# Closing the early tiles from the last recurrence unit on, none of them beside the last two own tiles

## The chip, the cores and the metric

One core of a Trainium2 chip runs the kernel. The metric is the device time of one execution in microseconds (us). Each engine works through its own list of instructions in order: TensorE (PE) multiplies matrices into PSUM, VectorE (DVE) does the elementwise work and the scans, ScalarE (ACT) moves PSUM into SBUF with a scale, GpSimd (POOL) and SyncE (SP) mostly issue DMAs here. Engines wait for each other through semaphores.

## The reference

For an input `x` of 2048 tokens by 1024 channels in bf16, two branches are computed and mixed with a gate per token:

```python
g = sigmoid((x * gate_w).sum(-1, keepdims=True))
# branch A: a filter in the two-dimensional Fourier domain
a = irfft2(rfft2(x) * (w_r + 1j * w_i), s=(2048, 1024))
# branch B: a diagonal complex recurrence over the tokens
Lam_bar = exp(exp(log_dt) * Lam)
Bu = einsum("bld,pd->blp", x, ((Lam_bar - 1) / Lam)[:, None] * Bmat)
h_t = Lam_bar * h_{t-1} + Bu_t
b = 2 * einsum("bld,pd->bld", h, Cmat).real + x * Dskip
out = g * a + (1 - g) * b
```

(The second einsum contracts the 1024 states with `Cmat`.) The output is bf16, 2048 by 1024.

## The kernel before

**Tokens.** The output is made in 16 tiles of 128 tokens, numbered 0 to 15. The recurrence runs in 8 chunks `c` of 256 tokens, so tile `tb` needs the states of chunk `tb // 2`. A chunk's states are handled in two units, `unit(c, 0)` and `unit(c, 1)`, of 512 states each.

**A unit** (lines 251 to 306) has two halves, real and imaginary. A half is 32 matmuls on PE into a PSUM tile `psu` (L299) and one cast by ACT into `h` (L301). Its weights are the transposed B matrix, in the eight SBUF tiles `BT0` to `BT7`: the units with q = 0 read `BT0` to `BT3`, those with q = 1 read `BT4` to `BT7`. After the second half a unit puts seven pieces of DVE work on a list: `turn_back` (L260, L261), `join` (L266, L267, L269), two scans (L273), `carry_on` (L279 to L281), `turn` (L285, L286) and `join_on` (L291, L292). Only after `join_on` may PE use the unit's states. The order on PE, DVE and ACT is the order in which the program emits instructions. A call `vector(us)` emits pieces from the list until that many microseconds of them are spent; so the calls to `vector` set where DVE's pieces stand among its other work. SP's and POOL's queues are put in order by the scheduler.

**Tiles 0 to 9** are "early": their branch B is computed while branch A is still under way, scaled by 1 - g and written as float32 to `y_scratch` in DRAM (`early`, L574 to L580). They are closed late in the program. `late_tile` (L603) calls `spectral` (L585), which makes branch A for the tile: 8 matmuls into a PSUM tile `ps_id` (L591), one scaling by ACT (L594), four additions by DVE (L596, L597, L599, L600). Then POOL issues a DMA that adds the tile's `y_scratch` onto the result in SBUF (L605), and SP stores the sum (L613). The function `close(keep)` emits the stores of all closed tiles but the last `keep`. Here the home of the sum of tile `tb` is the whole of `BT[tb % 4]`: its first half holds the sum, its second half holds `eo`, the intermediate result of the additions. There are four homes.

**Tiles 10 to 15** are "own": `own_tile` (L615) computes branch B after branch A is ready. Each has two halves `hf` of 512 channels; each half is 16 matmuls over the states (L560) and 4 for the `Dskip` term (L564). Between its halves the program makes branch A of the next own tile (`spectral`, with a home in the tile `raw`). Tiles 10 to 13 add branch A with one more matmul (L567), and ACT writes the output (L625), which SP stores (L626). In tiles 14 and 15 DVE does the scaling and the addition for each half (L632), and SP stores each half (L634). The outputs lie in `BT[4 + tb % 4]`.

**PSUM.** Two pools matter. `psU` has two buffers that `psu`, the early `ps_y` and `ps_id` take in turn; `psA` has two that `ps_y` and `ps_h` of the own tiles take in turn. A matmul that starts a new tile waits until the tile two before it in the same pool has been read out.

**The last stage** (lines 899 to 918). The units (6, 1), (7, 0) and (7, 1) run first. Then five DMA transposes load `x` for tiles 11 to 15 over the free part of `xQ` (L910). Then come own tiles 10 to 15, and after each half of tiles 10 to 14 one early tile is closed, tiles 0 to 9 in order: the last two, 8 and 9, after the two halves of tile 14. `close(1)` is called before each.

Of the kernel before, what the change touches and what calls it, by code (L numbers as in the profile page):

```python
# [20 lines left out]
D = 1024  # L21
# [85 lines left out]
def kernel(  # L107
# [75 lines left out]
    BT = [btp.tile([P, 2, 8, P], BF16, name=f"BT{jb}") for jb in range(8)]  # L183
# [60 lines left out]
    def halloc(shape, dtype):  # L244
        pool = hpool[hcount[0] % (NHA + NHB) >= NHA]
        hcount[0] += 1
        return pool.tile(shape, dtype, name="h")
# [3 lines left out]
    def unit(c, q):  # L251
        sh = [P, 2, 4, TC]
        u = halloc(sh, BF16)
        js = slice(4 * q, 4 * q + 4)
        bc = lambda i: tab[:, i:i + 1, js, :].to_broadcast(sh)
        tmps = {}

        def turn_back():
            su = up.tile(sh, BF16, name="su")
            nc.vector.tensor_mul(out=su, in0=u[:, ::-1], in1=bc(1))  # L260
            nc.vector.tensor_mul(out=u, in0=u, in1=bc(0))  # L261
            tmps["su"] = su

        def join():
            su = tmps["su"]
            nc.vector.tensor_add(out=u[:, 0], in0=u[:, 0], in1=su[:, 0])  # L266
            nc.vector.tensor_sub(out=u[:, 1], in0=su[:, 1], in1=u[:, 1])  # L267
            if c:
                nc.vector.tensor_add(out=u[:, :, :, 0], in0=u[:, :, :, 0], in1=carry[:, :, js])  # L269

        def scan(ri):
            seg = u[:, ri].rearrange("p j t -> p (j t)")
            nc.vector.tensor_tensor_scan(out=seg, data0=rz[:, js].rearrange("p j t -> p (j t)"), data1=seg,  # L273
                                         initial=0.0, op0=ALU.mult, op1=ALU.add)

        def carry_on():
            if c + 1 < NCH:
                gl = u[:, :, :, TC - 1]
                nc.vector.tensor_mul(out=ck[:, 0, :, js], in0=gl, in1=cTC[:, js].unsqueeze(1).to_broadcast([P, 2, 4]))  # L279
                nc.vector.tensor_mul(out=ck[:, 1, :, js], in0=gl[:, ::-1], in1=sTC2[:, :, js])  # L280
                nc.vector.tensor_add(out=carry[:, :, js], in0=ck[:, 0, :, js], in1=ck[:, 1, :, js])  # L281

        def turn():
            sg = up.tile(sh, BF16, name="sg", tag="su")
            nc.vector.tensor_mul(out=sg, in0=u[:, ::-1], in1=bc(3))  # L285
            nc.vector.tensor_mul(out=u, in0=u, in1=bc(2))  # L286
            tmps["sg"] = sg

        def join_on():
            sg = tmps["sg"]  # L290
            nc.vector.tensor_add(out=u[:, 0], in0=u[:, 0], in1=sg[:, 0])  # L291
            nc.vector.tensor_sub(out=u[:, 1], in0=u[:, 1], in1=sg[:, 1])  # L292
            hs[c, q] = u

        for ri in range(2):
            psu = pools["u"].tile([P, 4, TC], FP32, name="psu", tag="psu")
            for j in range(4):
                for d8 in range(8):
                    nc.tensor.matmul(psu[:, j, :], lhsT=BT[4 * q + j][:, ri, d8, :],  # L299
                                     rhs=xQ[:, d8, :, 16 * c:16 * (c + 1)], start=(d8 == 0), stop=(d8 == 7))  # L300
            nc.scalar.copy(out=u[:, ri].rearrange("p b (q j) -> p b q j", j=16),  # L301
                           in_=psu.rearrange("p b (j q) -> p b q j", j=16))
            if ri == 1:
                work.extend([(2.4, turn_back), (1.5, join), (2.3, lambda: scan(0)), (2.3, lambda: scan(1)),
                             (0.5, carry_on), (2.4, turn), (1.4, join_on)])
            yield 3.5
# [3 lines left out]
    def vector(us):  # L310
        owed[0] += us
        while work and owed[0] > 0:
            cost, piece = work.pop(0)
            piece()
            owed[0] -= cost
        if not work:
            owed[0] = min(owed[0], 0.0)
# [264 lines left out]
    own_home = lambda tb: raw[:, 2 * D * (tb % 2):2 * D * (tb % 2 + 1)]  # L582
    flat = lambda t: t.rearrange("p r j m -> p (r j m)")

    def spectral(tb, scale, home):  # L585
        ZT_t = fft["ZT"]
        pse = pools["u"].tile([P, 4, H], FP32, name="ps_id", tag="psu")
        for slot, (cls, ri) in enumerate(((0, 0), (1, 1), (0, 1), (1, 0))):
            for kb in range(2):
                i = 4 * cls + 2 * kb + ri  # L590
                nc.tensor.matmul(pse[:, slot, :], lhsT=ZT_t[:, i, tb, :], rhs=fft["Gi"][:, i, :],  # L591
                                 start=(kb == 0), stop=(kb == 1))
        part = home[:, 0:D].rearrange("p (s c n) -> p s c n", s=2, c=2)
        nc.scalar.activation(out=part.rearrange("p s c n -> p (s c) n"), in_=pse, func=ACT.Copy, scale=scale[:, tb:tb + 1])  # L594
        eo = home[:, D:2 * D].rearrange("p (c k) -> p c k", c=2)
        nc.vector.tensor_add(out=eo[:, :, 0:H], in0=part[:, 0], in1=part[:, 1])  # L596
        nc.vector.tensor_sub(out=eo[:, :, K - 1:H - 1:-1], in0=part[:, 0], in1=part[:, 1])  # L597
        ga = part.rearrange("p s c n -> p s (c n)")
        nc.vector.tensor_add(out=ga[:, 0], in0=eo[:, 0], in1=eo[:, 1])  # L599
        nc.vector.tensor_sub(out=ga[:, 1], in0=eo[:, 0], in1=eo[:, 1])  # L600
        return ga, eo

    def late_tile(tb):  # L603
        ga, _ = spectral(tb, gB, flat(BT[tb % 4]))
        nc.gpsimd.dma_start(out=ga, in_=y_dram[tb].rearrange("h p n -> p h n"), accum_op=ALU.add)  # L605
        closing.append((tb, ga))

# [2 lines left out]
    def close(keep):  # L610
        while len(closing) > keep:
            tb, ga = closing.pop(0)
            nc.sync.dma_start(out=out2[P * tb:P * (tb + 1), :], in_=ga.rearrange("p h n -> p (h n)"))  # L613
# [91 lines left out]
    gB = cpool.tile([P, 16], FP32, name="gB")  # L705
# [32 lines left out]
    def chain(*items):  # L738
        for item in items:
            yield from item  # L740

    def halves(gen, n):
        for _ in range(n):
            next(gen, None)
# [151 lines left out]
    ga = {}  # L896
    late = list(range(NEARLY))

    def own(tb):
        for v in own_tile(tb, ga.pop(tb)):  # L900
            if v == "half" and tb + 1 < 16:
                ga[tb + 1] = spectral(tb + 1, grat if tb + 1 < NSUM else gB, own_home(tb + 1))
            yield v

    ga[NEARLY] = spectral(NEARLY, grat, own_home(NEARLY))
    for _ in chain(unit(6, 1), unit(7, 0), unit(7, 1)):
        vector(4.0)
    for tb in range(NEARLY + 1, 16):
        xs[tb] = xQ.rearrange("p d (k j) m -> p (d k) (j m)", k=2)[:, tb].rearrange("p (d m) -> p d m", m=P)
        nc.sync.dma_start_transpose(out=xs[tb], in_=x[P * tb:P * (tb + 1), :])  # L910
    for tb, counts in ((10, (1, 1)), (11, (1, 1)), (12, (1, 1)), (13, (1, 1)), (14, (1, 1)), (15, (0, 0))):
        for _, n in zip(own(tb), counts):
            vector(4.0)
            for _ in range(n):
                close(1)
                late_tile(late.pop(0))
            if tb == 15:
                close(0)
    guard.__exit__(None, None, None)

# [29 lines left out]
```

## Time and profile before

| what | value |
|---|---|
| median of 5 runs | 356.61 us (355.51 to 361.84) |
| the profiled execution | 357.93 us |
| its span, first to last instruction | 356.1 us |
| mean granted TensorE clock | 0.993 |
| PE busy | 340.4 us (96%) |
| DVE busy | 292.6 us (82%) |
| ACT busy | 167.6 us (47%) |
| POOL busy | 34.2 us (10%) |

The span is what the views of the trace cover; 1.83 us of the profiled execution lie around it. PE is busy almost throughout, so what counts is where PE has to wait and what comes after its last matmul. In the forty slices of the page PE shows 9 tenths in nearly every slice up to the 39th and 2 tenths in the last one, which is 8.9 us long.

### The profile page before, as it was taken

What the parts mean: (1) busy time and instruction counts of PE and PEld (TensorE: products, weight loads), DVE (VectorE), ACT (ScalarE), POOL (GpSimd) and SP (SyncE); (2) the same over time, 40 slices, a digit from 0 to 9 for tenths busy, and PEclk for the clock granted to TensorE, in tenths of its full rate; (3) what the DMA queues carried; (4) which work ended last, traced back from release to release, by engine and by line L of the source; (5) the groups of instructions that cost most, each with busy time, mean ns of one, the idle gap of its engine ahead of it and who ended that gap; (6) DMA issues with size and microseconds to landing.
All of it is one profiled execution on the core that took longest, in us unless ns stands there. A gap on an engine that the chain in (4) does not pass through costs nothing.

```text
span 356.1 us, 6452 instructions
## 1 busy us (share of the span) xinstructions
PE 340.4 (96%) x2529; PEld 226.8 (64%) x2529; DVE 292.6 (82%) x477; ACT 167.6 (47%) x215; POOL 34.2 (10%) x66
## 2 busy tenths in 40 slices
PE   8989899899997999999999999999999999999992
PEld 4555476676966584747566665786958875655651
DVE  2659777999995999999999999969146999999850
ACT  3698668654232145657555541563533324434410
POOL 1372111200011000000000000000000000212420
PEclk9999999999999999999999999999999999999997
DMA  7999999997964047899999727844501024366795
GB/s 253 416 250 164 209 214 191 190 246 186 269 154 91 0 90 187 227 222 273 247 274 241 229 83 208 211 117 116 149 0 61 1 60 119 61 116 124 100 213 130
DMA packets 83742, 59.55 MB, mean 167 GB/s; under 512 B 54368, under 2 KB 74496, under 8 KB 83584
## 3 DMA queue, kind: packets, MB, share of 16 engines
q1 hardware_dynamic: 80400, 56.46, 62.1%
q0 software_dynamic: 3232, 2.67, 7.9%
q8 instruction: 20, 0.33, 0.4%
q14 instruction: 10, 0.08, 0.1%
q10 hardware_dynamic: 80, 0.01, 0.0%
HBM read 31.32 MB, written 17.84 MB: 138 GB/s over the span
## 4 chain that ended last, share of the span: by engine, by line
PE 68%; DVE 14%; DMA 8%; issue 3%; ACT 3%; SPq 1%; POOL 0%; ACTq 0%; DVEq 0%
PE ps_y L560 24%; PE psu L299 21%; PE ps_is L501 4%; PE ps_h L560 4%; PE ps_id L591 4%; DVE h L273 2%; PE ps_fd L334 2%; PE ps_s L452 2%; PE ps_is L477 2%; DMA G_sb<-c_G 2%; PE ps_is L476 2%; DMA col_scratch<-Acol 2%; DMA turn_scratch<-A 2%; PE ps_y L564 2%; DVE A L348 1%
## 5 line engine op out<-in xcount | busy, mean ns | idle before, releaser
L299 PE MATMUL psu<-xQ,BT 128*128 128x256 bf16 x1024 | 116.1, 273 | 3.7 <-ACT ye L578 2.4
L299 PEld LDWEIGHTS <-BT 128*128 128x128 bf16 x1024 | 100.2, 98 | 19.1 <-issue 4.5
L560 PE MATMUL ps_y<-CT,h 128*128 128x512 bf16 x448 | 101.4, 379 | 0.0
L560 PEld LDWEIGHTS <-h 128*128 128x128 bf16 x512 | 50.0, 98 | 55.3
L273 DVE TENSOR_TENSOR_SCAN h<-rz,h 128x1024 bf16<-128x1024 f32 x32 | 72.4, 2282 | 0.3
L301 ACT CAST h<-psu 128x1024 bf16<-128x1024 f32 x32 | 32.3, 1010 | 61.2 <-PE psu L299 61.2
L605 POOL DMA_DIRECT2D BT<-y_scratch x10 | 12.1, 1206 | 227.1 <-DMA out_dram<-BT 195.3
L334 PE MATMUL ps_fd<-G_sb,preT 128*128 128x512 bf16 x128 | 30.4, 379 | 2.1 <-ACT X L337 1.6
L260 DVE TENSOR_TENSOR su<-h,tab 128x2048 bf16<-128x2048 bf16 x16 | 19.6, 1223 | 14.0 <-ACT h L301 11.3
L578 ACT ACTIVATE ye<-ps_y,omg 128x512 f32<-128x512 f32 x20 | 12.6, 683 | 34.8 <-PE ps_y L564 22.7
L334 PEld LDWEIGHTS <-preT 128*128 128x128 bf16 x128 | 11.9, 97 | 15.5 <-issue 3.2
L454 ACT CAST X<-ps_s 128x1024 bf16<-128x1024 f32 x16 | 16.2, 1014 | 8.7 <-PE ps_s L452 8.7
L261 DVE TENSOR_TENSOR h<-h,tab 128x2048 bf16<-128x2048 bf16 x16 | 19.6, 1225 | 0.8
L337 ACT CAST X<-ps_fd 128x1024 bf16<-128x1024 f32 x16 | 16.2, 1013 | 8.4 <-PE ps_fd L334 8.4
L286 DVE TENSOR_TENSOR h<-h,tab 128x2048 bf16<-128x2048 bf16 x16 | 19.6, 1225 | 0.5
L285 DVE TENSOR_TENSOR sg<-h,tab 128x2048 bf16<-128x2048 bf16 x16 | 19.5, 1218 | 0.0
L503 ACT CAST ZT<-ps_is 128x1024 bf16<-128x1024 f32 x16 | 15.4, 1022 | 6.9 <-PE ps_is L501 3.5
L348 DVE CAST A<-ps_s 128x1024 bf16<-128x1024 f32 x10 | 12.2, 1222 | 6.2 <-PE ps_s L346 4.2
L646 ACT COPY xQ<-pt 128x1024 bf16<-128x1024 bf16 x16 | 15.9, 1019 | 2.3 <-PE pt L645 2.3
L479 ACT CAST C<-ps_is 128x1024 bf16<-128x1024 f32 x16 | 16.1, 1007 | 0.0
L591 PE MATMUL ps_id<-raw,ZT 128*128 128x256 bf16 x128 | 15.8, 273 | 0.0
L501 PE MATMUL ps_is<-KRS_sb,raw 128*128 128x128 bf16 x128 | 15.3, 311 | 0.0
(192 smaller groups left out, 403.9 us busy)
## 6 DMA issues: line engine op xcount, KB each, us to landing
y_scratch<-ye SPq DMA_DIRECT2D x20, 256.0 KB, 2.4
CT<-in_A_x_dram SPq DMA_DIRECT2D x8, 512.0 KB, 6.8
turn_scratch<-A SPq DMA_DIRECT2D x16, 256.0 KB, 3.4
Bb<-turn_scratch SPq DMA_DIRECT2D x16, 256.0 KB, 3.9
turn_scratch<-C SPq DMA_DIRECT2D x16, 256.0 KB, 3.0
raw<-turn_scratch SPq DMA_DIRECT2D x16, 256.0 KB, 3.7
Wb<-in_A_w_r_dram SPq DMA_DIRECT2D x32, 127.8 KB, 4.2
Wb<-in_A_w_i_dram SPq DMA_DIRECT2D x32, 127.8 KB, 3.6
```

What stands on the lines that cost most here:

```text
L260: nc.vector.tensor_mul(out=su, in0=u[:, ::-1], in1=bc(1))
L261: nc.vector.tensor_mul(out=u, in0=u, in1=bc(0))
L273: nc.vector.tensor_tensor_scan(out=seg, data0=rz[:, js].rearrange("p j t -> p (j t)"), data1=seg, initial=0.0, op0=ALU.mult, op1=ALU.add)
L285: nc.vector.tensor_mul(out=sg, in0=u[:, ::-1], in1=bc(3))
L286: nc.vector.tensor_mul(out=u, in0=u, in1=bc(2))
L299: nc.tensor.matmul(psu[:, j, :], lhsT=BT[4 * q + j][:, ri, d8, :], rhs=xQ[:, d8, :, 16 * c:16 * (c + 1)], start=(d8 == 0), stop=(d8 == 7))
L301: nc.scalar.copy(out=u[:, ri].rearrange("p b (q j) -> p b q j", j=16), in_=psu.rearrange("p b (j q) -> p b q j", j=16))
L334: nc.tensor.matmul(ps[:, cls, :], lhsT=preTs[j][:, 4 * cls + d4, :], rhs=G_sb[:, cls, d4, :], start=(d4 == 0), stop=(d4 == 3))
L337: nc.scalar.copy(out=X1.rearrange("p r (i c) -> p r i c", c=2), in_=ps.rearrange("p c (r i) -> p r i c", r=2))
L501: nc.tensor.matmul(pv[:, :, g::4], lhsT=Cq[:, g, P * kc:P * (kc + 1)], rhs=KRS_sb[:, 1, :], start=True, stop=True)
L560: nc.tensor.matmul(psy, lhsT=hs[c, jb // 4][:, ri, jb % 4, P * tq:P * (tq + 1)], rhs=CT[ri][:, jb, 512 * dh:512 * (dh + 1)], start=(i == 0 ...
L591: nc.tensor.matmul(pse[:, slot, :], lhsT=ZT_t[:, i, tb, :], rhs=fft["Gi"][:, i, :], start=(kb == 0), stop=(kb == 1))
```

## The change

The early tiles are closed sooner. One is closed after each half of `unit(7, 1)`, and one after each half of tiles 10 to 13; none is closed beside tiles 14 and 15. All ten are still closed in order.

The homes are smaller and there are six. A sum takes half of a `BT` tile: `BT0`, `BT1` and `BT2` have two slots each, and tile `tb` has slot `tb % 6`. The intermediate `eo` lies in one half of `BT3`, the halves being taken in turn. `close(2)` instead of `close(1)` is called before a tile is closed, and `close(0)` when no early tile is left. The instructions of `late_tile` and `spectral` are the same in kind, number and size.

In the emitted lists nothing differs before the second half of `unit(7, 1)`. From there on, each early tile stands two places earlier on PE, ACT and DVE. On DVE tiles 0 and 1 now stand before the pieces of `unit(6, 1)`'s `join_on` and after `unit(7, 0)`'s `turn_back`, and seven early tiles (0 to 6) instead of five stand before `join_on` of `unit(7, 1)`. The five transposes still stand ahead of all the stores in SP's queue. The end of that queue is below, each entry a store:

| | last stores in SP's queue, in order |
|---|---|
| before | tile 6, first half of 14, tile 7, second half of 14, tile 8, first half of 15, tile 9, second half of 15 |
| changed | tile 8, first half of 14, tile 9, second half of 14, first half of 15, second half of 15 |

```diff
--- before.py
+++ after.py
@@ -582,7 +582,7 @@
     own_home = lambda tb: raw[:, 2 * D * (tb % 2):2 * D * (tb % 2 + 1)]
     flat = lambda t: t.rearrange("p r j m -> p (r j m)")
 
-    def spectral(tb, scale, home):
+    def spectral(tb, scale, home, eo_home=None):
         ZT_t = fft["ZT"]
         pse = pools["u"].tile([P, 4, H], FP32, name="ps_id", tag="psu")
         for slot, (cls, ri) in enumerate(((0, 0), (1, 1), (0, 1), (1, 0))):
@@ -592,7 +592,7 @@
                                  start=(kb == 0), stop=(kb == 1))
         part = home[:, 0:D].rearrange("p (s c n) -> p s c n", s=2, c=2)
         nc.scalar.activation(out=part.rearrange("p s c n -> p (s c) n"), in_=pse, func=ACT.Copy, scale=scale[:, tb:tb + 1])
-        eo = home[:, D:2 * D].rearrange("p (c k) -> p c k", c=2)
+        eo = (home[:, D:2 * D] if eo_home is None else eo_home).rearrange("p (c k) -> p c k", c=2)
         nc.vector.tensor_add(out=eo[:, :, 0:H], in0=part[:, 0], in1=part[:, 1])
         nc.vector.tensor_sub(out=eo[:, :, K - 1:H - 1:-1], in0=part[:, 0], in1=part[:, 1])
         ga = part.rearrange("p s c n -> p s (c n)")
@@ -601,7 +601,8 @@
         return ga, eo
 
     def late_tile(tb):
-        ga, _ = spectral(tb, gB, flat(BT[tb % 4]))
+        slot = lambda i: flat(BT[i // 2])[:, D * (i % 2):D * (i % 2 + 1)]
+        ga, _ = spectral(tb, gB, slot(tb % 6), slot(6 + tb % 2))
         nc.gpsimd.dma_start(out=ga, in_=y_dram[tb].rearrange("h p n -> p h n"), accum_op=ALU.add)
         closing.append((tb, ga))
 
@@ -903,18 +904,27 @@
             yield v
 
     ga[NEARLY] = spectral(NEARLY, grat, own_home(NEARLY))
-    for _ in chain(unit(6, 1), unit(7, 0), unit(7, 1)):
+    last = unit(7, 1)
+
+    def close_early(n):
+        for _ in range(n):
+            close(2)
+            late_tile(late.pop(0))
+
+    for _ in chain(unit(6, 1), unit(7, 0)):
         vector(4.0)
+    for n in (1, 1):
+        halves(last, 1)
+        vector(4.0)
+        close_early(n)
     for tb in range(NEARLY + 1, 16):
         xs[tb] = xQ.rearrange("p d (k j) m -> p (d k) (j m)", k=2)[:, tb].rearrange("p (d m) -> p d m", m=P)
         nc.sync.dma_start_transpose(out=xs[tb], in_=x[P * tb:P * (tb + 1), :])
-    for tb, counts in ((10, (1, 1)), (11, (1, 1)), (12, (1, 1)), (13, (1, 1)), (14, (1, 1)), (15, (0, 0))):
+    for tb, counts in ((10, (1, 1)), (11, (1, 1)), (12, (1, 1)), (13, (1, 1)), (14, (0, 0)), (15, (0, 0))):
         for _, n in zip(own(tb), counts):
             vector(4.0)
-            for _ in range(n):
-                close(1)
-                late_tile(late.pop(0))
-            if tb == 15:
+            close_early(n)
+            if not late:
                 close(0)
     guard.__exit__(None, None, None)
```

## The prediction

> **What bounds the kernel now.** I read the view of the chain that ended last first, restricted to the last 15 us. Its columns are start, length, engine, tile and line.
>
> ```profile
> 340.86 0.87 PE ps_id L591 x8
> 341.74 3.45 PE ps_h L560 x16
> 345.19 0.22 PE ps_h L564 x4
> 345.41 3.45 PE ps_h L560 x16
> 348.87 0.24 PE ps_h L564 x4
> 349.10 0.02 issue
> 349.13 0.75 DVE BT L632
> ```
>
> PE works without a gap that matters: from 269.02 on each piece of this chain begins where the last ended, to a few tenths. Then comes DVE's last addition, done at 349.13 + 0.75 = 349.88. But the span is 356.1. The timeline of SP and of POOL for the same stretch shows what fills the other 6.2 us.
>
> ```profile
> 336.30 1.20 POOL L605 DMA_DIRECT2D BT<-y_scratch  x1 [0.27 <-issue]
> 341.08 1.20 POOL L605 DMA_DIRECT2D BT<-y_scratch  x1 [3.59 <-DVE BT L600]
> 346.10 1.20 POOL L605 DMA_DIRECT2D BT<-y_scratch  x1 [3.82 <-DVE BT L600]
> ...
> 343.63 0.33 SPq L613 DMA_DIRECT2D out_dram<-BT  x1
> ...
> 347.24 0.33 SPq L613 DMA_DIRECT2D out_dram<-BT  x1
> ...
> 352.64 0.33 SPq L613 DMA_DIRECT2D out_dram<-BT  x1
> 353.07 0.39 SPq L634 DMA_DIRECT2D out_dram<-BT  x1
> ```
>
> The last accumulating DMA (tile 9) is issued at 346.10, and its store goes out at 352.64, 6.54 later. The store of tile 15's second half stands behind it in SP's queue and goes out at 353.07, 3.19 us after its data was ready. From there 3.03 us remain to the end: 2.0 until the store lands (the shortest landing listed for L634), the rest the program's closing. The view of SP's own waits names the cause.
>
> ```profile
> SPq L613 <- DMA BT<-y_scratch: 44.1, 10, 7.5
> ```
>
> So two things set the end: PE's list up to 349.1, and one accumulation that ends after PE does.
>
> **Step 1, the tail.** In the changed list SP's last three entries are the halves of tiles 14 and 15, with no early store between or behind. The last store can start when its data is ready. Handing over from an engine to SP costs about 0.03 us where SP's queue is clear (ACT's L625 of tile 10 ended at 300.82, its store started at 300.85). Saved: 3.19 - 0.03 = **3.16 us**, if tile 9's sum is stored by then (step 4).
>
> **Step 2, a new wait on PE.** Before, the two halves of `unit(7, 1)` took different buffers of `psU`. Now tile 0's `ps_id` stands between them, so the second half takes the buffer of the first half again and must wait for ACT's cast of it. The trace has no such wait in this stretch, so I build it from rows. ACT's cast of this half is this one, in the timeline of ACT:
>
> ```profile
> 286.69 1.01 ACT L301 CAST h<-psu 128x1024 bf16<-128x1024 f32 x1 [2.48 <-PE psu L299]
> ```
>
> By the chain the half ends at 269.02 + 5 x 3.49 = 286.47, so ACT starts 0.22 later and needs 1.01. PE goes on some 0.05 after ACT is done (ACT ended at 268.97, PE began at 269.02). That is 1.28 us. Tile 0's 8 matmuls cover 0.87 of it. Left: **0.4 us** of stall, and everything on PE behind it is as much later. Its ends: 0, if the cast is not waited for, and 1.28, if the 8 matmuls hide nothing. I take 0.4, since all three terms are rows.
>
> No other `ps_id` waits: its buffer was read out a unit half (3.5 us) or an own half (3.67 us) earlier, and ACT needs 1.1.
>
> **Step 3, DVE.** This is the part that could turn the result, since DVE has no room: in 279 to 290 it is busy 10.69 of 11 us, and from 300 to 330 97 to 98%. No operation is added. But two more early tiles stand before `join_on` of the last unit. One costs 1.45 us of DVE (tile 0: its four additions start at 301.32, the next operation at 302.77). DVE's one gap before, 0.43 us at 296.09, is filled by this. So the last unit's states come 2 x 1.45 - 0.43 = 2.47 us later: L292 starts at 329.17 and takes 0.68, so 329.85 becomes 332.3. They are first needed by the 9th matmul of tile 14. PE starts that tile at 331.76, and 8 matmuls of 0.216 make 333.49. PE is later here too, by two groups of `ps_id` moved ahead of it (2 x 0.87) and the 0.4: 2.15 us in all, so the states are needed at 335.6. 3.3 us of room are left, against 3.6 before. Cost: nothing; if the cover were gone, each further us of delay would be a us of PE.
>
> The next in line is the read-out of `ps_h`. DVE reached L632 of tile 14's first half at 335.70 after eight early tiles. With ten it gets there at 335.70 + 2.47 = 338.2, while PE has the half ready at 335.44 + 2.15 = 337.6. So this read-out comes 0.6 us late and is over at 338.9. Who waits for its buffer is the first half of tile 15, which PE starts at 341.74 + 0.4 = 342.1. Nothing is lost. After it DVE has only tile 15's branch A and three more L632 to do.
>
> **Step 4, the accumulations and the homes.** POOL issues 0.5 us after the four additions. Before, tiles 5, 6 and 7 were issued at 331.83, 334.83 and 336.30; in the changed list tiles 7, 8 and 9 take just these places, 2.47 later: 334.3, 337.3, 338.8. The stores behind the old ones went out at 337.6, 340.18 and 343.63, so the longest took 7.3 us. Tile 9's sum is then ready at 338.8 + 7.3 = 346.1. The last store's data comes at 349.88 + 0.4 = 350.3. So 4.2 us are to spare, and SP stores the second half of 14 and the first half of 15 (ready at about 346.6) in between.
>
> Here a rule of the Trainium skill speaks against the change. "DMA: Bandwidth & Descriptors", section "Anatomy of one DMA — SWDGE (gpsimd) path", fits a DMA from GpSimd as about 2.0 us plus its bytes by 436 GB/s. For the 512 KB of float32 that a tile reads this gives an estimate of 3.2 us: tile 9 would have landed at 349.3 in the kernel before, ahead of the last addition at 349.88. There would be no tail to take away, and the change would only bring its stall, +0.4. The rows say 5.35 to 7.3 us, and SP's store at 352.64 shows it where it matters. I go by the rows.
>
> As for homes, a slot is written again six tiles later. ACT's scaling for tile 6 waits until tile 0 is stored: tile 0 is added by DVE until 293.2, issued at 293.7, landed by 301.0, stored by 303.3 (a 256 KB store lands in 2.3). Tile 6 comes to ACT after 316. Tile 9 waits for tile 3 the same way, with some 12 us between. Before, the last-but-one early tile did wait 4.4 us for its home (ACT L594), off the path; that goes and brings nothing.
>
> Tiles 0 and 1 are accumulated while the five transposes of `x` run, which start 1.3 us later than before (0.87 + 0.4), at 291.2. The transposes land 3.4 us after issue, and the first one is needed by L564 of tile 11, at about 303.8 + 2.15. Ten us of cover.
>
> **The sum.** -3.16 + 0.4 = -2.76 us. The span goes from 356.1 to 353.3, the profiled execution from 357.93 to 355.2. The median of the runs shown lies 1.32 under the profiled execution; with the same saving it goes from 356.61 to **353.8 us**. The stall's ends give 353.45 and 354.7.
>
> **Rivals.**
>
> *A: the accumulations still hold the tail.* In 330 to 346 the DMA engines' busy share was 0.85 to 1.08, so they are full, and tiles 8 and 9 are issued 1.5 us apart. If tile 9's sum is ready later than 349.9, the last store waits again; the end is that moment plus 0.43 and 3.03. At 12 us of landing (350.8) the median would be 354.8; from 352.6 (13.8 us) on, no gain is left: 356.6. For it: the full engines, and the rise from 5.35 to 7.3 in the one pair issued so closely. Against it: nearly twice the worst row is needed, and the three issues have the spacing of a trio that is in the trace. Chance 9%.
>
> *B: slower, because DVE becomes the bound in the last unit.* The mechanism: the additions now write `eo` into another tile than they read, and if that form ran slower, seven early tiles' worth of it, 28 additions, would stand before the last states. It decides from 3.3 us of delay on, and makes the kernel slower when the delay passes 3.3 + 2.76 = 6.1 us, that is at 0.22 more for each addition over the 0.42 of today. At twice today's 0.42 the delay would be 11.8, the stall 8.5 and the median **362.3**. The nearest slower row, DVE's cast of 128x1024 from PSUM in 1222 ns, makes 0.61 for 512 columns: 5.3 us of delay, 2 of stall, 355.9, no change that can be measured. For it: DVE's load of 98%. Against it: shapes, types and strides are the same, and `join_on` (L291, 128x1024 in 0.68) already runs between two tiles with no such penalty. Chance 7%.
>
> **How the numbers follow.** The forecast has 84%. About 0.3%, 1.1 us, is what a measurement of this kernel can tell from no change. All of the forecast lies under 355.5, so faster; of A's 9% I give 2 to faster, 5 to no change, 2 to slower; of B's 7% all but 1 to slower. Together 0.86, 0.06, 0.08. The range: the lower end is 353.45 less about 0.6 for the spread of the runs (355.5 to 356.7 but for one); the upper end takes the stall's far end, 354.7, and the middle of A. That makes 352.9 to 355.2.
>
> **What would show it.** In the profile after: the last L614, the store of an early tile, at about 346 and the last store at about 350.3, at once after DVE's last addition; PE waiting 0.4 us for ACT's cast once, between the halves of the last unit, and nowhere behind; L292 of the last unit over at about 332.3, with PE's tile 14 begun at 333.9 and no wait in it; POOL's issues of tiles 8 and 9 some 1.5 us apart near 337 and 339. The prediction is wrong if PE waits for DVE in tile 14, if the last early store goes out after 350, or if the last addition ends later than 350.6.

## The result and the profile after

The changed kernel takes 352.75 us (median of 44 runs, 352.08 to 358.77), against 356.67 us for the kernel before (79 runs beside it, 354.42 to 363.69). The ratio is 0.9921, with a 95% interval of 0.9904 to 0.9939: 2.8 us of 356. The forecast was 353.8 from 356.61; the measured ratio makes 353.8 of that too. Executions of one kernel differ by several us, since some are disturbed (those of the profiles e2, e2b and e6 below are among them): undisturbed ones alone enter the ratios, and small differences are read from one stage of the profiles.

The span fell from 356.1 to 351.2 us, which is more. To see what belongs to the change I count from the first matmul of `unit(6, 1)` to the end of the span and call that the **last stage**; it holds all that the change touches. It began at 269.02 before and begins at 267.24 now. (Spans are printed to 0.1 us, so the end of a stage is good to 0.05.) Those 1.78 us arose ahead of the first difference between the two lists of instructions. The last stage itself went from 87.08 to 83.96: **3.12 us** less.

The chain that ended last, in the changed kernel (start, length, engine, tile, line; lines behind the edit are numbered one higher, so L633 is the former L632):

```profile
335.80 0.87 PE ps_id L591 x8
336.67 3.45 PE ps_h L560 x16
340.12 0.22 PE ps_h L564 x4
340.35 3.45 PE ps_h L560 x16
343.80 0.22 PE ps_h L564 x4
344.02 3.45 PE ps_h L560 x16
347.48 0.24 PE ps_h L564 x4
347.71 0.02 issue
347.74 0.75 DVE BT L633
```

As before, PE runs without a gap into DVE's last addition. What follows is shorter. The timeline of POOL and of SP, same kernel:

```profile
335.21 1.20 POOL L606 DMA_DIRECT2D BT<-y_scratch  x1 [1.80 <-DVE BT L600]
336.67 1.20 POOL L606 DMA_DIRECT2D BT<-y_scratch  x1 [0.26 <-issue]
...
344.33 0.33 SPq L614 DMA_DIRECT2D out_dram<-BT  x1
...
348.51 0.33 SPq L635 DMA_DIRECT2D out_dram<-BT  x1
```

Tile 9, the last accumulation, is issued at 336.67 and stored at 344.33. The last store goes out at 348.51, 0.02 after the last addition ended (347.74 + 0.75), where it had waited 3.19 before. From there 2.69 us remain, against 3.03: this store landed in 1.7 us where the other took 2.0 with a 256 KB store issued 0.43 ahead of it. The pattern holds over the profiles below: 3.03 to 3.05 us remain in the four with such a store just ahead (before, e2, e2b, e3), 2.7 to 2.8 in those where the last store goes out alone. The tail went from 6.22 to 2.71.

The one loss stands at the start of the stage, in PE's timeline, first before and then changed:

```profile
269.02 21.12 PE L299 MATMUL psu<-xQ,BT 128*128 128x256 bf16 x192 [0.53 <-ACT ye L578]
```

```profile
267.24 17.63 PE L299 MATMUL psu<-xQ,BT 128*128 128x256 bf16 x160 [0.53 <-ACT ye L578]
284.71 1.04 PE L591 MATMUL ps_id<-raw,ZT 128*128 128x256 bf16 x8
285.97 3.65 PE L299 MATMUL psu<-xQ,BT 128*128 128x256 bf16 x32 [0.23 <-ACT h L301]
```

Before, these 192 matmuls were one row. Now tile 0's 8 stand between, and PE then waits for ACT's cast (bracket of the last row). The bracket shows 0.23, but the modelled end of the row ahead hides a part: the last addition starts 80.50 us into the stage where it was 80.11, so the cost is 0.39. Sum: -3.51 + 0.39 = -3.12.

### The profile page after: what moved, and what is told of

It is laid out like the page before. It is cut to its first block, busy times and chain, and to the rows that moved or that the text cites. A ratio compares the mean times of both kernels' runs of the same rounds, so it can differ in the third digit from the quotient of the medians.

```text
span 351.2 us, 6441 instructions
## 1 busy us (share of the span) xinstructions
PE 339.5 (97%) x2529; PEld 225.9 (64%) x2529; DVE 292.1 (83%) x477; ACT 167.5 (48%) x215; POOL 34.4 (10%) x66
## 4 chain that ended last, share of the span: by engine, by line
PE 79%; DVE 6%; SPq 4%; ACT 4%; issue 3%; DMA 3%; ACTq 0%; DVEq 0%
PE psu L299 28%; PE ps_y L560 26%; PE ps_is L501 4%; PE ps_h L560 4%; SPq L204 4%; PE ps_id L591 3%; PE ps_fd L334 3%; PE ps_is L477 2%; PE ps_s L452 2%; PE ps_is L476 2%; DMA G_sb<-c_G 2%; PE ps_y L564 2%; ACT h L301 1%; ACT xQ L647 1%; DVE A L348 1%
```

## The experiments

Times in us from the start of the last stage, from one profile each (the stage's own begin is from the start of the span); the ratio is to the kernel before.

| kernel | stage begins | tile 9 issued | tile 9 stored | last addition starts | stage ends | ratio (95%) |
|---|---|---|---|---|---|---|
| before | 269.02 | 77.08 | 83.62 | 80.11 | 87.08 | 1 |
| changed | 267.24 | 69.43 | 77.09 | 80.50 | 83.96 | 0.9921 (0.9904 to 0.9939) |
| a2_changed | 267.38 | 69.46 | 77.32 | 80.49 | 84.02 | 0.9922 (0.9890 to 0.9953) |
| e1_place_only | 265.98 | 69.44 | 77.71 | 80.49 | 84.02 | 0.9882 (0.9843 to 0.9920) |
| e2_homes_only | 272.68 | 75.97 | 83.54 | 80.10 | 87.02 | 0.9956 (0.9917 to 0.9996) |
| e2b_homes_only | 272.30 | 75.97 | 82.44 | 80.11 | 85.90 | 0.9977 (0.9941 to 1.0013) |
| e3_last_back | 266.34 | 76.35 | 82.29 | 80.49 | 85.76 | 0.9935 (0.9901 to 0.9970) |
| e4_shift_one | 266.12 | 72.93 | 80.36 | 80.11 | 84.18 | 0.9904 (0.9850 to 0.9957) |
| e5_two_stalls | 268.02 | 69.84 | 77.91 | 80.88 | 84.38 | 0.9779 (0.9710 to 0.9849) |
| e6_dve_two | 272.21 | 71.98 | 80.36 | 80.49 | 84.59 | 0.9841 (0.9755 to 0.9928) |
| e7_dve_five | 266.76 | 75.77 | 83.17 | 85.73 | 89.24 | 1.0061 (1.0023 to 1.0099) |
| e8_other_pool | 266.05 | 69.45 | 76.69 | 80.11 | 83.65 | 0.9922 (0.9891 to 0.9952) |
| e9_dve_three | 267.16 | 73.23 | 82.26 | 81.63 | 86.44 | 0.9976 (0.9945 to 1.0007) |

In e2, e2b and e6 the stage began some 5 us later than in the others; only the last stage is read there. The ratios of e5 and e6 come from four runs each and lie below that of the changed kernel, although both stages are longer; they can't rank these kernels.

### Places alone

```diff
-        slot = lambda i: flat(BT[i // 2])[:, D * (i % 2):D * (i % 2 + 1)]
-        ga, _ = spectral(tb, gB, slot(tb % 6), slot(6 + tb % 2))
+        ga, _ = spectral(tb, gB, flat(BT[tb % 4]))
...
-            close(2)
+            close(1)
```

> Only the new places of the early tiles, with the four old homes and stores two tiles behind. I measure the last stage, from the first matmul of unit (6, 1) to the end of the span: 87.1 us in the kernel before, 84.0 after the change. Theory (the place alone takes the tail away): 84.0 again, and the time of the changed kernel, ratio to before about 0.992. Rival (the six homes are needed, since ACT waits for a home with four): a wait of ACT of about 4 us on a store comes back, early sums land later, and the last stage is 85 or more.

Measured: 84.02, as the changed kernel. The view of ACT's waits shows none for a store. The places alone bring the whole gain; in these places four homes do as well as six.

### Homes alone

```diff
-    for _ in chain(unit(6, 1), unit(7, 0)):
+    for _ in chain(unit(6, 1), unit(7, 0), last):
         vector(4.0)
-    for n in (1, 1):
-        halves(last, 1)
-        vector(4.0)
-        close_early(n)
...
-(14, (0, 0)), (15, (0, 0))):
+(14, (1, 1)), (15, (0, 0))):
```

> Only the six homes and close(2), with the early tiles in their old places. Theory (homes matter only through the one wait of ACT seen before: it held the scaling of tile 9 until 342.89, while its matmuls were done at 341.57): tile 9 is issued by POOL 1.1 us sooner, and as it still holds the end, the last stage is 86.0 instead of 87.1, ratio about 0.997. Rival, which is what my prediction said (the wait is off the path and brings nothing): 87.1, ratio 1.000. Rival (homes carry the gain): 84.

> The six homes in the old places once more, since the profile of the first run fell into a disturbed execution. Theory: POOL issues tile 9 at 76.0 us into the last stage as then (77.1 before), its sum takes 6.5 and not 7.6, last stage 86.0, ratio 0.997. Rival (sums land when the DMA engines are done with what is queued, however soon they are issued): store of tile 9 at 83.6 again, last stage 87.0, ratio 1.000.

The row of ACT that I had set aside as off the path, in the timeline of ACT of the kernel before:

```profile
342.89 1.11 ACT L594 ACTIVATE BT<-ps_id,gB 128x1024 bf16<-128x1024 f32 x1 [4.37 <-DMA out_dram<-BT]
```

This is tile 9, the very tile whose sum came last. With six homes it waits for its matmuls only (e2b, timeline of ACT):

```profile
345.05 1.11 ACT L594 ACTIVATE BT<-ps_id,gB 128x1024 bf16<-128x1024 f32 x1 [3.26 <-PE ps_id L591]
```

It starts 72.75 us into the stage instead of 73.87, and POOL issues the tile at 75.97 instead of 77.08, in both runs. What that is worth differs: in e2b the store goes out 6.47 after the issue and the stage ends 1.2 sooner, in e2 it goes out 7.57 after and nothing is gained. In both, tile 8's sum, still under way, took longer: 8.75 us (e2) and 7.63 (e2b) from issue to store, against 6.16 before; that fits the second rival. The ratios, 0.9956 (0.9917 to 0.9996) and 0.9977 (0.9941 to 1.0013), both allow the 0.997 of my theory, and the second allows no gain as well; the fastest runs are only 0.05 and 0.59 us under the fastest of the kernel before beside them. So what the homes alone are worth in the old places stays open, 0 to 1.2 us by the profiles: one of them supports my theory, the other the rivals that say no gain.

### One tile put back

```diff
-(13, (1, 1)), (14, (0, 0)), (15, (0, 0))):
+(13, (1, 0)), (14, (0, 1)), (15, (0, 0))):
```

> The changed kernel, but tile 9 alone stands again beside the second half of tile 14. Theory (the tail is this one accumulation in front of the last store): POOL issues it about 76.3 us into the last stage, its store goes out about 82.6, the last store at 83.0 and the last stage takes 86.1, 2.1 more than the changed kernel; ratio about 0.998. Rival (the gain comes from the whole shift, from less crowded DMA engines at the end): most of it stays, 84.5 or less.

Measured: 85.76, 1.8 more than the changed kernel. POOL's and SP's timelines:

```profile
342.69 1.20 POOL L606 DMA_DIRECT2D BT<-y_scratch  x1 [7.16 <-DVE BT L600]
...
348.63 0.33 SPq L614 DMA_DIRECT2D out_dram<-BT  x1
349.06 0.38 SPq L635 DMA_DIRECT2D out_dram<-BT  x1
```

The pair of the kernel before is back: an early store and, 0.43 behind it, the last one, 1.48 after its data was ready (346.83 + 0.75). Nine of ten tiles still stand two places earlier, and the store still waits: the tail hangs on this one accumulation. The plain times of this round agree: the fastest run took 353.66 us, that of e1 351.77. The ratio, 0.9935, is further from 1 than the 0.998 expected; its interval does not reach that. To the kernel before, 1.3 us are missing: tile 9 is issued 0.73 sooner (the wait for its home is gone, less the 0.39 on PE), and its store leaves 5.94 after the issue instead of 6.54. Less crowded DMA engines, the rival, can thus account for 0.6 at most.

### One place instead of two

```diff
-    for n in (1, 1):
+    for n in (0, 1):
         halves(last, 1)
...
-(14, (0, 0)), (15, (0, 0))):
+(14, (1, 0)), (15, (0, 0))):
```

> The early tiles are moved by one place only: tile 0 after both halves of unit (7, 1), tile 9 beside the first half of tile 14. Theory: no ps_id stands between the halves of the unit, so PE's wait for the cast (0.4 us) goes; tile 9 is issued by POOL about 72.1 us into the stage and stored about 78.3, before the last store at 80.9: last stage 83.6, 0.4 less than the changed kernel, ratio to before about 0.991. Rival (one accumulation beside tile 14 is already too late): the last store waits and the stage takes over 84.5.

PE's wait is gone and the last addition starts at 80.11. But the stage takes 84.18, no less than the changed kernel's 83.96. SP's timeline shows why:

```profile
346.48 0.33 SPq L614 DMA_DIRECT2D out_dram<-BT  x1
346.91 0.88 SPq L635 DMA_DIRECT2D out_dram<-BT  x2
```

Tile 9 was issued at 72.93 and not 72.1, and its sum took 7.43 us from its issue and not the 6.2 I reckoned with; either miss alone would have left the store in time. Its store leaves at 346.48, both halves of tile 15 queue behind it, and the second, ready at 346.98, goes out at about 347.4. The 0.4 gained on PE is lost in SP's queue.

### The wait on PE, twice and not at all

Twice, in e5:

```diff
     for n in (1, 1):
+        close_early(n)
         halves(last, 1)
         vector(4.0)
-        close_early(n)
```

> The changed kernel with tiles 0 and 1 ahead of the two halves of unit (7, 1) instead of behind them, so that a ps_id stands between unit (7, 0) and unit (7, 1) too. Theory: the wait of PE for ACT's cast comes twice; last stage 84.4 instead of 84.0. Rival (the wait in the changed kernel is chance, or hidden by PE's own queue): 84.0.

Not at all, in e8:

```diff
-        pse = pools["u"].tile([P, 4, H], FP32, name="ps_id", tag="psu")
+        pse = psA.tile([P, 4, H], FP32, name="ps_id", tag="ps") if eo_home is not None and tb == 0 else pools["u"].tile([P, 4, H], FP32, name="ps_id", tag="psu")
```

> The changed kernel, with tile 0's ps_id in the pool psA, which is free until tile 10, so that the halves of unit (7, 1) take different buffers of psU again. Theory (the wait between the halves is the buffer's): no wait of PE there, the last addition starts 80.1 us into the last stage instead of 80.5, last stage 83.6 instead of 84.0, ratio to before about 0.991. Rival (the wait moves to the next tile that needs a buffer): 84.0.

The last addition starts at 80.88 with two waits, 80.50 with one, 80.11 with none: 0.39 each. In PE's timeline of e8 the bracket is gone:

```profile
266.05 17.63 PE L299 MATMUL psu<-xQ,BT 128*128 128x256 bf16 x160 [0.53 <-ACT ye L578]
284.39 3.66 PE L299 MATMUL psu<-xQ,BT 128*128 128x256 bf16 x32
```

e8 ends its stage at 83.65, the shortest of all, 0.3 under the changed kernel. That it beats it the timings can't say: 0.9922 for both, measured on the same chip.

### How much room DVE has

```diff
-            nc.vector.tensor_mul(out=su, in0=u[:, ::-1], in1=bc(1))
+            for _ in range(3 if (c, q) == (7, 1) else 1):
+                nc.vector.tensor_mul(out=su, in0=u[:, ::-1], in1=bc(1))
```

(3 in e6, 6 in e7, 4 in e9.)

> The changed kernel with the first DVE product of unit (7, 1) (128x2048, 1.26 us from start to start) done three times, with the same result: 2.5 us more DVE work before the last states. Theory (DVE has 3.4 us of room there): last stage 84.0, no change. Rival (DVE already bounds the stage): 84.0 plus up to 2.5.

> The same with the product done six times: 6.3 us more. Theory: 6.3 less 3.4 of room is 2.9 us of PE waiting for DVE at the 9th matmul of tile 14, last stage 86.9, about the time of the kernel before. Rival (the room is larger, since DVE can catch up elsewhere): 84 to 85.

> The changed kernel with the first DVE product of unit (7, 1) done four times, 3 x 1.26 = 3.8 us more. New theory, from the run with five more: the room is 2.7 us and ends at L567 of tile 13, which waits for the additions of tile 13's branch A (done at 322.53 in the profile of the changed kernel, needed at 325.23); so PE waits 3.8 - 2.7 = 1.1 us there, the granted clock stays at 1.0 since the wait is short, the last addition starts 81.6 us into the last stage instead of 80.5. Rival, the step of my prediction (room of 3.4 us up to the 9th matmul of tile 14): a wait of 0.4, 80.9. Third, if what follows the wait in the other run was no effect of its length: half the clock again, and 83 or more.

With 2.5 us more work PE doesn't wait at all: the last addition of e6 starts at 80.49 (its stage is longer all the same, which is taken up below). With 6.3 us more it starts 5.23 late, where I expected 2.9. The PE timeline of e7 and its table by stretches (length, busy time of PE, PEld, DVE, ACT and POOL with their instructions, granted clock, DMA share, GB/s):

```profile
324.52 0.39 PE L565 MATMUL ps_y<-dgD,xQ 128*128 128x128 bf16 x4
328.43 0.59 PE L568 MATMUL ps_y<-raw,ident 128*128 128x512 bf16 x1 [3.52 <-DVE raw L600]
328.81 3.30 PE L592 MATMUL ps_id<-raw,ZT 128*128 128x256 bf16 x16
```

```profile
328.00:329.00 1.00, 0.57 (x2) 0.25 (x2) 1.00 (x3) 0.00 (x0) 0.88 (x1) 0.61 0.30 111
329.00:330.00 1.00, 1.00 (x7) 0.73 (x5) 1.00 (x1) 0.00 (x0) 0.00 (x0) 0.50 1.00 350
330.00:331.00 1.00, 1.00 (x7) 0.69 (x6) 1.00 (x2) 0.19 (x1) 0.00 (x0) 0.50 0.99 103
331.00:332.00 1.00, 1.00 (x7) 0.78 (x7) 0.97 (x4) 0.92 (x1) 0.00 (x0) 0.68 0.96 98
332.00:333.00 1.00, 0.95 (x5) 0.44 (x5) 1.00 (x3) 0.85 (x1) 0.13 (x1) 1.00 1.03 119
```

Two things are new. First, PE waits not in tile 14 but earlier, at the matmul that adds tile 13's branch A (L568 here, the former L567): DVE makes that branch A behind the delayed pieces. In the changed kernel the same two rows stand at

```profile
322.10 0.43 DVE L599 TENSOR_TENSOR raw<-raw 128x512 bf16<-128x512 bf16 x1
```

```profile
325.23 0.38 PE L567 MATMUL ps_y<-raw,ident 128*128 128x512 bf16 x1
```

DVE is done at 322.10 + 0.43 = 322.53, so the room is 325.23 - 322.53 = 2.7 us, and 6.3 - 2.7 = 3.6 is the wait, 3.52 in the bracket. Second, the granted clock falls to half behind that wait. A slice of 1 us with a mean clock of 0.61 spent 0.78 us at half; so the rows make 0.78 + 1.00 + 1.00 + 0.64 = 3.4 us at half clock, from about 328.2 on, 3.3 us after PE's last matmul had ended (324.52 + 0.39 = 324.91). The 16 `ps_id` matmuls take 3.30 instead of 1.91 and L568 0.59 instead of 0.38, which is the rest of the 5.23, 1.6 us. The Trainium skill, "TensorE: Matmul & The Clock Gate", section "What's actually happening", halves the clock after an idle window of about 3.4 us, until a busy one has passed; the 3.3 and 3.4 us here agree with it. The delay is not the same each time, though: behind its last matmul the kernel before shows the fall after 2.0 us (349.1 to 351.1), and e9 shows none in the 4.8 us to its end. So these runs give no length of wait from which the clock falls.

e9 was made to test both. Its wait in PE's timeline:

```profile
326.29 0.38 PE L568 MATMUL ps_y<-raw,ident 128*128 128x512 bf16 x1 [0.98 <-DVE raw L600]
326.50 1.91 PE L592 MATMUL ps_id<-raw,ZT 128*128 128x256 bf16 x16
```

A wait of 1.0 at the same matmul, no slower matmuls behind it, and the last addition at 81.63, where 81.6 was expected. The room of 2.7 is confirmed, and behind this shorter wait the clock stays at 1.00.

The end shows a third thing, here in POOL's and SP's timelines of e9:

```profile
340.39 1.20 POOL L607 DMA_DIRECT2D BT<-y_scratch  x1 [0.26 <-issue]
...
349.42 0.33 SPq L615 DMA_DIRECT2D out_dram<-BT  x1
349.84 1.38 SPq L636 DMA_DIRECT2D out_dram<-BT  x3
```

A delay on DVE also delays the accumulations: tile 9 is issued 2.55 us later in e6 and 3.8 later in e9. In e9 it then took 9.03 us from issue to store, in e6 8.38; in both the last three stores stood behind it in SP's queue. So e6 ended at 84.59 and e9 at 86.44, 0.6 and 2.5 over the changed kernel, of which PE's own delay explains 0 and 1.1. The 84.0 expected of e6 was missed for this reason.

### The changed kernel once more

> The changed kernel itself, for comparison on the same chip. Theory: last stage 84.0, the start of unit (6, 1) anywhere between 266 and 269; ratio 0.992. Rival (the change also sped up the front, where the first profile began the last stage 1.8 us sooner than before): it begins at 267.2 again.

84.02, the same last stage. It began at 267.38; the kernels with the same front began it between 265.98 and 268.02 (e2, e2b and e6 left aside). I have one profile of the kernel before, at 269.02, so whether the front differs at all stays open. The last stage alone, 3.1 us, is as much as the ratio gives.

## Why the prediction was right

- **The number.** The forecast of 353.8 is met more closely than the terms behind it. Their sum was 2.76 us, the last stage gives 3.12, and the interval of the ratio reaches from 2.2 to 3.4; that the median agrees to 0.1 is in part luck.
- **The tail (step 1).** Right in mechanism: 3.16 was reckoned, 3.51 measured. The rest, 0.34, is a term held fixed at 3.03 from the store's issue to the end. It was 2.69; it is 2.7 to 2.8 wherever the last store goes out alone. e3 shows that tile 9's accumulation alone makes the tail.
- **The wait on PE (step 2).** 0.4 reckoned, 0.39 measured, and 0.39 for each further one (e5, e8). The sum of three rows, cast plus hand-over less what covers it, held.
- **DVE (step 3).** It costs nothing, as said: tile 14 began 64.71 us into the stage (64.73 reckoned), and the last unit's states were ready at 62.99 (63.28). But the room was named wrongly. "They are first needed by the 9th matmul of tile 14 ... 3.3 us of room" is true of the states, yet the additions of tile 13's branch A stand in the same line of DVE, and their room is 2.7. The accumulations have less still: 2.5 us of delay cost 0.6 at the end with no wait of PE (e6), and 3.8 us cost 2.5 (e9). Rival B counted neither; nor did it count the half clock behind PE's long wait in e7. With 6.3 us added, where B's sum comes out about even, the stage was 2.2 us longer than before (0.6 for the smaller room, 1.6 for the clock), and the ratio was 1.0061.
- **The accumulations (step 4).** The store of tile 9 was reckoned at 77.1 us into the stage and went out at 77.09. Two errors cancel there: the issue came 0.35 sooner, at 69.43, and the sum took 7.66, over the 7.3 named as the longest. Over all profiles with two accumulations issued 1.5 us apart at the end, the later one took 7.2 to 9.0 until its store. The spare 4.2 us were there (348.49 - 344.33), but e6 and e9 show that 2.5 to 4 us of delay use them up: with that delay the last store waits as rival A had it. In the changed kernel A did not come true. Its "so they are full" was read from means: from 332 to 334 the DMA engines' share was 0.20.
- **The rule set against the rows.** The estimate of 3.2 us that step 4 made from the skill's fit would have left no tail. The change won 3.5 there, and no accumulation in any of these profiles landed in under 5 us. The measurement decides. That the adding makes the difference is not shown: POOL's DMAs of 8 KB and less earlier in the kernel before, which add nothing, took 4.4 to 7.2 us to land.
- **The homes.** "Off the path" was wrong for the kernel before: the tile that waited 4.4 us was not the last but one, it was the last, and its sum was the path. "Brings nothing" is open there (e2 and e2b differ). It holds in the changed kernel, since in the new places the wait doesn't arise (e1).

## What to carry to other kernels

A queue that serves in order lets a late small job hold back the job that ends the program: look at what stands ahead of the last store, and when its input was issued, before counting an engine's busy time. When work is moved ahead of other work on a full engine, list everything behind it in that engine's order, not only the item whose readiness was asked for, and follow each to the transfers that it starts; the shortest room decides. And a wait of one instruction ahead of a slow transfer is on the path if that transfer is.

## What was not expected of the hardware

An accumulating DMA from GpSimd of 512 KB of float32 landed in 5.1 to 7.3 us before. Tile 9's took 7.2 to 9.0 until its store where it was issued 1.5 us after tile 8's, but also 7.4 in e4 and 7.6 in e2, where it was issued 4.7 and 3.9 us after; what sets it stays open. A wait of PE of 1.0 us made the end of its work 1.1 later (e9); one of 3.5 us made it 5.2 later (e7), since the clock was at half for some 3 us of the work behind it.
